# Attention with decay and a mixing layer: last tokens of two heads scored with a shared operand, and GpSimd's order fixed by more edges

## The chip, the cores and the metric

One core of a Trainium2 chip runs the whole program. Five engines work side by side, each through its own instructions in order: TensorE (PE in the profile; its weight loads are PEld), VectorE (DVE), ScalarE (ACT), GpSimd (POOL) and SyncE (SP, which here only issues DMAs). They hand work to each other by semaphores. The metric is the device time of one execution in microseconds; the kernel before has a median of 1192.06 us over three runs (1191.97 to 1192.15).

## The reference

Eight batches, eight heads, 576 tokens, head size 64. First attention with a decay for each head, then a mixing layer over tokens, then a two-layer network, all in f32:

```
scores = q @ k.T / 8                      # per batch and head, 576 x 576
cum    = cumsum(log(clip(f, 1e-4, 1)))    # per batch and head, 576
scores = where(causal, -1e9, scores + cum[:, None] - cum[None, :])
attn   = softmax(scores) ; x = attn @ v   # heads side by side: (8, 576, 512)
u      = x + (U V mixing over the 576 tokens)
out    = u + relu(u @ w_ch1) @ w_ch2      # 512 -> 2048 -> 512
```

A softmax row does not change when a constant is added to the row.

## The kernel before

**Numbers.** Products that need f32 accuracy are either one f32 matmul (pairs 0 to 5) or split into a rounded high part and a low part (f32r), and several f32r matmuls are added in one bank.

**The pair loop (9 to 643 us of the profile).** Two heads of a batch are a pair; there are 32 pairs. `step(t)` scores pair p = t, turns the probabilities of pair t-1 and multiplies them with values, and finishes pair t-2. A step has ten slots. Slots 0 to 3 score the first head (j = 0) in four blocks of 128 queries (`score`, 128 to 512 keys), slots 4 and 5 score the last 64 queries of both heads together in two halves of 288 keys (`score_tail`, HW = 288), the end of slot 6 to slot 9 score the second head (j = 1). Each score goes through VectorE (`top`: mask and negated maximum, L388 and L414) and ScalarE (`use`: exponential, L396 and L424). From pair NF = 6 on, a step also carries pieces of the mixing layer and of the first six of 16 chunks of the two-layer network (`filler`). After the loop the other ten chunks follow, which nothing here touches.

**Operands of the scores.** For pairs 0 to 5, q and k lie in `padded` tiles: rows 0 to 63 the head, two more rows the decay, the rest zero. `qk_mm` makes one f32 matmul of it (L364). From pair 6 on, tile G[j] (128 rows, 4 chunks, 640 columns) holds head j: chunk 0 the rounded q (L367 multiplies it with chunk 2, rounded k with the low part of k in the other rows), chunk 1 the low part of q with the decay of the queries in four rows, chunk 3 the rounded k with the decay of the keys (L368). `parts(p, j)` writes G[j]: two casts of 128x576 (ScalarE, in the step of a mix GpSimd), a cast of 64x576 (L330), and two subtractions of 64x576 on GpSimd, L345 (low part of k) and L346 (low part of q). G[0] for the next pair is written from slot 6, G[1] from slot 0. `place_decay` sends the decay rows by DMA (L351) at slot 7 for j = 0, at slot 0 for j = 1. `score_tail` puts four matmuls into a bank in each half: L367 and L368 for each head.

**Who sets the order.** TensorE and SyncE run in the order of the program text in most of the loop; VectorE, ScalarE and GpSimd in an order that a planner gives them, with extra edges by `behind` (a dependency without a semaphore). `at(phase, fn)` puts work into this slot, `defer(phase, fn, n)` n slots later, both ahead of the slot's loads and matmuls. On SyncE a DMA that waits holds all that is behind it.

**Mixing.** After the last pair of a batch, ten units (`mix_units`) run over one step: five `hmix`, four `tu` (transposes of the mixed tokens, split into uh and ul), one `tv`. For batches 1 to 6, `tu(2)` and `tu(3)` are staged: ScalarE copies the block to `full`, and GpSimd casts and subtracts it two slots later (L688, L689). Three slots after `tv`, uh and ul (1 MB each) are stored to `ud` for the sweep after the loop; odd batches store 256 KB more of each. `make_vs` splits the values, its low part on GpSimd (L199). `split_x` splits x (L630, L631 on GpSimd).

Of the kernel before, what the change touches and what calls it, by code (L numbers as in the profile page):

```python
# [21 lines left out]
P = 128  # L22
# [16 lines left out]
NF = 6  # L39


@with_exitstack
def tile_decay_attention_moe(ctx, tc, qk, v, f, U, V, w1, w2, out):
# [4 lines left out]
    accd = nc.dram_tensor("accd", (NG, NM, P, DM), F32, kind="Internal").ap()  # L48

# [5 lines left out]
    def behind(ins, kind):  # L55
        tc.add_manual_dep(
            ins.ins, newest[kind].ins.name,
            mybir.DependencyInfo(mybir.DependencyClass.NoSync, mybir.DependencyReason.DATA), reason=f"order behind {kind}",
        )
# [68 lines left out]
    mask = att.tile([P, ZR + HW], F32, name="mask")  # L128
    nc.vector.memset(mask, 0.0)
# [12 lines left out]
    def clear_operands():  # L142

        for j in range(2):
            g = G[j].bitcast(F32)
            tc.keep_in_program_order(nc.gpsimd.memset(g[OTH[j], 1, COLS[j]], 0.0))
            tc.keep_in_program_order(nc.gpsimd.memset(g[OTH[j], 3, COLS[j]], 0.0))
            tc.keep_in_program_order(nc.gpsimd.memset(g[ORW[j] : ORW[j] + 4, 1, COLS[j]], 1.0))
            tc.keep_in_program_order(nc.gpsimd.memset(g[ORW[j] : ORW[j] + 4, 3, COLS[j]], 1.0))
# [4 lines left out]
    def decay_log():  # L154
        fr = sb.tile([B * H, S], F32, tag="xT", name="fr")
        fl = sb.tile([B * H, S], F32, tag="cr", name="fl")
        return fr, fl, G[0][0 : B * H, :, 0:S], sb.tile([B * H, 2, S], F32, tag="VS", name="dq")
# [36 lines left out]
    def split(dh, dl, src, heng, leng):  # L194
# [4 lines left out]
        leng.tensor_tensor(dl, src, dh.bitcast(F32), op=ALU.subtract)  # L199
# [12 lines left out]
    def load_w(u):  # L212
# [4 lines left out]
        if kind == "w2":  # L217

            spare = xn[NX - 1].rearrange("p c d -> p (c d)").bitcast(I32)
            if fc % 2:  # L220
                raw, a = spare[:, 1536:2560], sb.tile([P, 512], I32, tag="w2a", name=f"stg{u}")
# [101 lines left out]
    def make_vs(p):  # L323
# [3 lines left out]
        split(VS[:, :, :, 0:D], VS[:, :, :, D:P], vr, nc.scalar, nc.gpsimd)  # L327
# [4 lines left out]
    def parts(p, j, engines):  # L332
# [46 lines left out]
    def score(p, j, i):  # L379
# [7 lines left out]
        def top():  # L387
            newest["top"] = nc.vector.tensor_tensor_reduce(  # L388
                ps[:, :w], ps[:, :w], mask[:, 512 - w : 512], scale=-SCALE, scalar=3.0e38,
                op0=ALU.add, op1=ALU.min, accum_out=z["nm"][:, col : col + 1],  # L390
            )

# [12 lines left out]
    def score_tail(p, x):  # L405
# [160 lines left out]
    def values(p, j):  # L566
# [7 lines left out]
        z["cr"] = sb.tile([D, S], F32, tag="cr", name=f"cr{p}_{j}")  # L574
# [1135 lines left out]
```

## Time and profile before

| | us |
|---|---|
| median of three runs | 1192.06 |
| profiled execution | 1192.27 |
| its span, first to last instruction | 1190.5 |
| TensorE busy | 1173.5 (99%) |
| VectorE, ScalarE, GpSimd busy | 906.1, 752.7, 561.1 |
| granted TensorE clock, mean | 1.000 of full |
| bytes moved | 138.47 MB, 116 GB/s |

Busy time counts from an instruction's start to its end; TensorE's matmuls overlap, so what one costs is read from the distance between starts. A timeline row gives start, length, engine, line, operation, output<-inputs and how many were merged; in brackets the idle time of the engine ahead of it and what ended it. The chain that ended last lies on TensorE for 85% of the span, on VectorE for 8%, on ScalarE for 4%.

### The profile page before, as it was taken

The numbers are of one execution on the slowest core, as the hardware profiler recorded it, in microseconds if no ns is written. First come the engines' busy times: TensorE is split into PE (matmuls) and PEld (weight loads), VectorE is DVE, ScalarE is ACT, GpSimd is POOL, SyncE is SP. The second block draws the span as 40 slices with busy tenths as digits, with TensorE's granted clock in tenths as the row PEclk, the third lists the DMA queues.
The fourth block names the chain that finished last, engine by engine and source line by source line (L and its number), as shares of the span: only waits on it lengthen the run. The fifth ranks groups of instructions, "written<-read, shape, count | busy, mean of one in ns | idle before, by whom it ended". The sixth has DMA issues, their size and how long they took to land.

```text
span 1190.5 us, 23774 instructions
## 1 busy us (share of the span) xinstructions
PE 1173.5 (99%) x8400; PEld 1080.8 (91%) x8400; DVE 906.1 (76%) x2188; ACT 752.7 (63%) x2046; POOL 561.1 (47%) x588
## 2 busy tenths in 40 slices
PE   8999999999999999999999999999999999999998
PEld 5888899999899989989989997788999999999998
DVE  8988777677777677777676699966777767777675
ACT  8887786766868758767765577344454544545443
POOL 3315565546637447555553000024565555555554
PEclk9999999999999999999999999999999999999999
DMA  5754234434426425426332344542424344243421
GB/s 161 196 147 153 78 98 146 116 82 142 121 74 174 114 58 163 111 74 179 82 84 96 108 142 155 155 112 95 131 89 124 97 135 138 94 107 102 130 54 36
DMA packets 81431, 138.47 MB, mean 116 GB/s; under 512 B 8768, under 2 KB 46144, under 8 KB 79264
## 3 DMA queue, kind: packets, MB, share of 16 engines
q1 hardware_dynamic: 79680, 128.16, 36.1%
q0 software_dynamic: 1152, 8.39, 3.8%
q8 instruction: 66, 1.08, 0.4%
q14 instruction: 53, 0.43, 0.1%
q10 hardware_dynamic: 480, 0.40, 0.1%
HBM read 101.08 MB, written 35.78 MB: 115 GB/s over the span
## 4 chain that ended last, share of the span: by engine, by line
PE 85%; DVE 8%; ACT 4%; issue 2%; POOL 1%; DMA 0%; SPq 0%; ACTq 0%; DVEq 0%; POOLq 0%
PE N L1321 12%; PE B L775 12%; PE A L756 11%; PE A L1301 9%; PE B L1301 7%; PE V L579 6%; PE T L467 4%; PE S L367 3%; PE S L368 3%; PE O L1402 2%; PE B L1321 2%; PE V L544 2%; PE Tt L645 2%; PE S L364 1%; PE T_v L485 1%
## 5 line engine op out<-in xcount | busy, mean ns | idle before, releaser
L396 ACT ACTIVATE P<-S,nm 128x128 f32<-128x128 f32 (+3 forms) x256 | 138.0, 541 | 53.7 <-DVE nm L388 52.7
L199 POOL TENSOR_TENSOR hb<-xn,hb 128x256 fp32r<-128x256 f32 x136 | 111.6, 840 | 126.3 <-ACT hb L196 113.4
L388 DVE CUSTOM_DVE_ANT_0 S<-S,mask 128x128 f32<-128x128 f32 (+3 forms) x256 | 125.7, 497 | 52.5 <-PE S L368 48.6
L330 POOL CAST G<-qk 64x576 fp32r<-64x576 f32 (+1 forms) x76 | 50.6, 679 | 172.4 <-PE St L368 63.8
L756 PE MATMUL A<-uh,w1h 128*128 128x256 f32 (+1 forms) x384 | 119.8, 312 | 0.0
L756 PE MATMUL A<-ul,w1h 128*128 128x256 f32 (+1 forms) x384 | 113.6, 296 | 0.0
L756 PE MATMUL A<-uh,w1l 128*128 128x256 f32 (+1 forms) x384 | 113.5, 296 | 0.0
L196 ACT CAST hb<-xn 128x256 fp32r<-128x256 f32 x136 | 51.7, 404 | 84.7 <-DVE xn L1307 45.5
L775 PE MATMUL B<-w2h,hh 128*128 128x512 f32 x216 | 88.2, 408 | 0.0
L446 DVE TENSOR_TENSOR PTl<-T,PTh 128x512 fp32r<-128x512 f32 (+1 forms) x156 | 78.4, 527 | 9.6 <-ACT PTh L443 8.6
L467 PE MATMUL T<-ident,P 128*128 128x128 f32 x544 | 85.3, 272 | 0.0
L775 PE MATMUL B<-w2l,hh 128*128 128x512 f32 x216 | 85.0, 394 | 0.0
L775 PE MATMUL B<-w2h,hl 128*128 128x512 f32 x216 | 84.6, 392 | 0.0
L1321 PE MATMUL N<-sw,hb 128*128 128x256 f32 x546 | 79.9, 282 | 0.0
L1321 PE MATMUL N<-b2h,hb 128*128 128x256 f32 x420 | 79.8, 282 | 0.0
L345 POOL TENSOR_TENSOR G<-qk,G 64x576 fp32r<-64x576 f32 x52 | 74.7, 1437 | 10.8 <-issue 4.1
L346 POOL TENSOR_TENSOR G<-qk,G 64x576 fp32r<-64x576 f32 x52 | 75.0, 1442 | 6.6 <-ACT G L330 5.0
L367 PE MATMUL S<-G 128*128 128x128 f32 x208 | 70.9, 345 | 4.5 <-ACT P L396 3.3
L756 PEld LDWEIGHTS A<-uh,w1h 128*128 128x128 f32 x384 | 72.9, 190 | 0.9 <-DVE hl L761 0.2
L756 PEld LDWEIGHTS A<-uh,w1l 128*128 128x128 f32 x384 | 73.1, 190 | 0.5
L756 PEld LDWEIGHTS A<-ul,w1h 128*128 128x128 f32 x384 | 72.9, 190 | 0.0
L1321 PEld LDWEIGHTS N<-sw,hb 128*128 128x128 f32 x546 | 71.6, 190 | 0.0
(342 smaller groups left out, 3995.1 us busy)
## 6 DMA issues: line engine op xcount, KB each, us to landing
qk<-in_qk_dram SPq DMA_DIRECT2D x104, 288.0 KB
direct<-ud SPq DMA_DIRECT2D x48, 256.0 KB
sr<-in_w_dram SPq DMA_DIRECT2D x20, 512.0 KB
vr<-in_v_dram SPq DMA_DIRECT2D x32, 256.0 KB
accd<-ost SPq DMA_DIRECT2D x32, 256.0 KB
xn<-accd SPq DMA_DIRECT2D x8, 1024.0 KB
out_dram<-xn SPq DMA_DIRECT2D x30, 256.0 KB
ud<-uh SPq DMA_DIRECT2D x7, 1024.0 KB
```

The source lines that it names most:

```text
L199: leng.tensor_tensor(dl, src, dh.bitcast(F32), op=ALU.subtract)
L345: pin(el.tensor_tensor(g[oth, 2, cols], k[oth], gf[oth, 2, cols], op=ALU.subtract))
L346: pin(em.tensor_tensor(g[own, 1, cols], q[own], gf[own, 0, cols], op=ALU.subtract))
L367: nc.tensor.matmul(ps, G[j][:, 0, c0 : c0 + P], G[j][:, 2, cols], start=first, stop=False)
L388: newest["top"] = nc.vector.tensor_tensor_reduce(ps[:, :w], ps[:, :w], mask[:, 512 - w : 512], scale=-SCALE, scalar=3.0e38, op0=ALU.add, o ...
L396: nc.scalar.activation(pt, ps[:, :w], AF.Exp, bias=z["nm"][:, col : col + 1], scale=-1.0, accum_out=z["sm"][:, col : col + 1])
L446: defer(2, lambda: nc.vector.tensor_tensor(dstl, src, dsth.bitcast(F32), op=ALU.subtract))
L467: nc.tensor.transpose(tp[:, P * x : P * x + P], z["P"][j][i][:, P * c : P * c + P], ident)
L756: nc.tensor.matmul(ps[:, :nt], wt[:, fc, c], ut[:, c, sl], start=m == 0, stop=m == 3 * NDC - 1)
L775: nc.tensor.matmul(ps, ht[:, fc, P * x : P * x + P], wt[:, fc], start=fc == 0 and m == 0, stop=fc == NA - 1 and m == 2,)
L1301: nc.tensor.matmul(ps, a[x][:, c], b[y][:, c], start=start and m == 0, stop=m == 5, skip_group_check=not start)
L1321: nc.tensor.matmul(ps[:, y], a[p_][:, P * y : P * y + P], w[q_], start=start and y == 0 and m == 0, stop=stop and y == 1 and m == 2,)
```

## The change

Six edits, all within the pair loop and what prepares it.

1. *Last tokens, pairs 6 to 31.* One matmul less per half. For each head the rounded q meets chunk 2 as before (two matmuls). The two products of the low parts of q become one: `join_keys` copies, by two DMAs at slot 0, head 0's rounded k into the other rows of G[1]'s chunk 3, and head 0's low q of the last tokens into chunk 1 beside head 1's. The decay rows of head 1's keys are overwritten by this; `place_decay` parks them in four spare rows of G[0] (`ASIDE`), and `next_decay` has GpSimd copy them over in slots 5 and 6, when the last tokens are scored.
2. *Last tokens, pairs 4 and 5.* `join_tail` has GpSimd put both heads' q and k into `both_q` and `both_k` (four copies), and one f32 matmul per half replaces two.
3. *Their decay.* From pair NO = 4 on the decay of the last tokens' keys comes in with the mask that VectorE adds: `based` (in DRAM, made once) holds -8 (cum - cum[511]); `load_tail` sends it to 64 rows for each head at slot 8 of the step before, and `lean_mask` has GpSimd add the causal part of the last 64 columns at slot 2. The decay of the queries, a constant in each row, is left out.
4. *Order on GpSimd.* `parts` notes its two subtractions as "lows"; the low part of VS and the casts of the staged blocks are put behind them. The staged blocks come 5 and 9 slots after their copy instead of 2 and 2.
5. *Stores.* uh and ul are stored 10 slots after `tv` instead of 3.
6. *Value sum.* `joined` (VectorE's sum of the two value halves) is put ahead of the maximum of the first head's second block (slot 1).

The tiles of the preparation change places with this (`fr`, `fl`, the staged w2 weights), the mask grows by 288 columns, and five of the ten memsets of `clear_operands` fall away. The core of the diff:

```diff
     def behind(ins, kind):
-        tc.add_manual_dep(ins.ins, newest[kind].ins.name, ...)
+        found = newest[kind]
+        for x in found if isinstance(found, tuple) else (found,):
+            tc.add_manual_dep(ins.ins, x.ins.name, ...)
...
     def make_vs(p):
-        split(VS[:, :, :, 0:D], VS[:, :, :, D:P], vr, nc.scalar, nc.gpsimd)
+        low = split(VS[:, :, :, 0:D], VS[:, :, :, D:P], vr, nc.scalar, nc.gpsimd)
+        if p < NP - 1:
+            behind(low, "lows")
...
     def parts(p, j, engines):
-        pin(el.tensor_tensor(g[oth, 2, cols], k[oth], gf[oth, 2, cols], op=ALU.subtract))
-        pin(em.tensor_tensor(g[own, 1, cols], q[own], gf[own, 0, cols], op=ALU.subtract))
+        low = pin(el.tensor_tensor(g[oth, 2, cols], k[oth], gf[oth, 2, cols], op=ALU.subtract))
+        last = pin(em.tensor_tensor(g[own, 1, cols], q[own], gf[own, 0, cols], op=ALU.subtract))
+        newest["lows"] = low, last
+
+    def load_tail(p):
+        if not NO <= p < NP:
+            return
+        for j in range(2):
+            r = j * B * NHP + p
+            nc.sync.dma_start(lean[64 * j : 64 * j + 64], based[r : r + 1].broadcast_to([64, S]))
+
+    def join_tail(p):
+        if not NO <= p < NF:
+            return
+        for j in range(2):
+            q, k = st[p]["qk"][j]
+            at = AOFF[1] if j else MAIN
+            nc.gpsimd.tensor_copy(both_q[OWN[j], 64 * j : 64 * j + TAIL], q[0:64, at : at + TAIL])
+            nc.gpsimd.tensor_copy(both_k[OWN[j]], k[0:64])
+
+    def lean_mask(p):
+        if NO <= p < NP:
+            nc.gpsimd.tensor_tensor(lean[:, MAIN:S], lean[:, MAIN:S], tri, op=ALU.add)
+
+    ASIDE = slice(96, 100)
+
+    def next_decay(lo, hi):
+        nc.gpsimd.tensor_copy(G[1][0:4, 3, AOFF[1] + lo : AOFF[1] + hi], G[0].bitcast(F32)[ASIDE, 3, lo:hi])
+
+    def join_keys():
+        g, h = (x.bitcast(F32) for x in G)
+        nc.sync.dma_start(h[OTH[1], 3, COLS[1]], g[OWN[0], 3, COLS[0]])
+        nc.sync.dma_start(h[OTH[1], 1, 0:TAIL], g[OWN[0], 1, MAIN:S])
 
     def place_decay(p, j, cm=None):
-            nc.sync.dma_start(G[j].bitcast(F32)[o : o + 4, 1:4:2, COLS[j]], cumd[r])
+            g = G[j].bitcast(F32)
+            if j == 0:
+                nc.sync.dma_start(g[o : o + 4, 1:4:2, 0:MAIN], cumd[r][:, :, 0:MAIN])
+                nc.sync.dma_start(g[ASIDE, 3, 0:MAIN], cumd[B * NHP + p][:, 1, 0:MAIN])
+            else:
+                nc.sync.dma_start(g[o : o + 4, 1, P:], cumd[r][:, 0, TAIL:S])
...
     def score(p, j, i):           # in top()
+            if (j, i) == (0, 1) and "joined" in newest:
+                behind(ins, "joined")
...
     def score_tail(p, x):
-        for j in range(2):
-            qk_mm(ps[:, :hw], p, ATAIL[j], cols, j == 0, j == 1, j)
+        if p < NO:
+            for j in range(2):
+                qk_mm(ps[:, :hw], p, ATAIL[j], cols, j == 0, j == 1, j)
+        elif p < NF:
+            nc.tensor.matmul(ps[:, :hw], both_q, both_k[:, cols], start=True, stop=True)
+        else:
+            at = [slice(AOFF[j] + cols.start, AOFF[j] + cols.stop) for j in range(2)]
+            for j in range(2):
+                nc.tensor.matmul(ps[:, :hw], G[j][:, 0, ATAIL[j] : ATAIL[j] + P], G[j][:, 2, at[j]], start=j == 0, stop=False)
+            nc.tensor.matmul(ps[:, :hw], G[1][:, 1, 0:P], G[1][:, 3, at[1]], start=False, stop=True)
-                ps[:, :hw], ps[:, :hw], mask[:, x * ZR : x * ZR + hw], scale=-SCALE,
+                ps[:, :hw], ps[:, :hw], lean[:, hw * x : hw * x + hw], scale=-SCALE,
...
     def evac_u(dh, dl, src, late):
-                    nc.gpsimd.tensor_copy(dh, whole)
+                    behind(nc.gpsimd.tensor_copy(dh, whole), "lows")
-                defer(6, parts_of, 2)
+                defer(6, parts_of, 5 if late == 1 else 9)
...
     def tv():                     # the stores of uh and ul
-            defer(7, use, 3)
+            defer(7, use, 10)
...
     def step(t):
             if s == 0 and ps_ and p >= NF:
                 place_decay(p, 1)
+                join_keys()
+            if s == 2 and ps_:
+                at(5, lambda: lean_mask(p))
+            if s == 5 and ps_ and p >= NF:
+                at(5, lambda: next_decay(0, HW))
+            if s == 6 and ps_ and p >= NF:
+                at(5, lambda: next_decay(HW, MAIN))
+            if s == 9 and ps_:
+                at(5, lambda: join_tail(p + 1))
+            if s == 8 and ps_:
+                load_tail(p + 1)
```

## Rows read from the trace of the kernel before

**Rows 1.** The page: span, and busy time of TensorE, share, instructions.
```profile
span 1190.5 us, 23774 instructions
...
PE 1173.5 (99%) x8400; PEld 1080.8 (91%) x8400; DVE 906.1 (76%) x2188; ACT 752.7 (63%) x2046; POOL 561.1 (47%) x588
```

**Rows 2.** Busy us by step: length, PE, PEld, DVE, ACT, POOL, clock, DMA share, GB/s.
```profile
62.53:77.83 15.30, 15.30 (x110) 12.84 (x108) 14.36 (x43) 12.03 (x37) 1.92 (x3) 1.00 0.51 149
...
303.74:322.44 18.70, 18.70 (x122) 16.69 (x121) 14.07 (x43) 15.01 (x44) 11.11 (x11) 1.00 0.38 98
...
sum 633.61, PE 625.05 PEld 564.46 DVE 487.12 ACT 472.70 POOL 326.48; mean PE 19.53 PEld 17.64 DVE 15.22 ACT 14.77 POOL 10.20
```

**Rows 3.** What TensorE waited for: us, times, longest.
```profile
PE S L367 <- ACT P L396: 3.3, 5, 1.1
```

**Rows 4.** Timeline of TensorE (start, us, what), one step: last-token scores.
```profile
312.15 0.29 PE L367 MATMUL St<-G 128*128 128x288 f32 x1
...
312.68 0.27 PE L507 MATMUL Ty<-ident,Ptl 128*64 128x128 f32 x1
...
317.08 0.22 PE L367 MATMUL S<-G 128*128 128x128 f32 x1
```

**Rows 5.** Timeline of TensorE, step of pair 4.
```profile
67.97 1.13 PE L364 MATMUL St<-qk 128*128 128x288 f32 x4
68.94 0.27 PE L507 MATMUL Ty_None<-ident,Ptl 128*64 128x128 f32 x1
```

**Rows 6.** Instructions of line 367: min/median/max ns.
```profile
L367 PEldq EVENT_SEMAPHORE  x26: 51/51/51, 90.4 to 621.1; - x26
```

**Rows 7.** Timeline of SyncE's issues.
```profile
298.43 6.16 SPq L351 DMA_DIRECT2D G<-cumd  x2
304.64 1.18 SPq L294 DMA_DIRECT2D qk<-in_qk_dram  x2
```

**Rows 8.** Engines and DMA (last two: share, GB/s) during a store of uh.
```profile
287.50:291.00 3.50, 3.50 (x29) 3.33 (x28) 3.02 (x9) 2.66 (x10) 3.42 (x3) 1.00 0.98 333
```

**Rows 9.** DMA issues: count, KB each, us to landing where it shows.
```profile
ud<-uh SPq DMA_DIRECT2D x7, 1024.0 KB
...
xn<-ud POOLq DMA_DIRECT2D x7, 1024.0 KB, 8.3
```

**Rows 10.** Timeline of GpSimd, a step after mixing and a plain one.
```profile
299.17 1.43 POOL L345 TENSOR_TENSOR G<-qk,G 64x576 fp32r<-64x576 f32 x1
...
313.39 0.66 POOL L330 CAST G<-qk 64x576 fp32r<-64x576 f32 x1 [4.33 <-PE St L368]
...
315.62 1.29 POOL L631 TENSOR_TENSOR xl<-xn,xh 128x512 fp32r<-128x512 f32 x1
...
318.61 1.43 POOL L345 TENSOR_TENSOR G<-qk,G 64x576 fp32r<-64x576 f32 x1
```

**Rows 11.** Timeline of VectorE, plain step.
```profile
306.52 0.43 DVE L388 CUSTOM_DVE_ANT_0 S<-S,mask 128x256 f32<-128x256 f32 x1
...
307.04 0.75 DVE L599 TENSOR_TENSOR xT<-V,cr 64x576 f32<-64x576 f32 x1
```

**Rows 12.** Timeline of GpSimd, a mixing step and the start of the next.
```profile
276.00 1.88 POOL L330 CAST G<-qk 128x576 fp32r<-128x576 f32 x3 [9.91 <-PE St L367]
...
278.49 1.29 POOL L631 TENSOR_TENSOR xl<-xn,xh 128x512 fp32r<-128x512 f32 x1
...
286.09 1.29 POOL L689 TENSOR_TENSOR ul<-full,uh 128x512 fp32r<-128x512 f32 x1
```

**Rows 13.** Timeline of GpSimd, the step after mixing of an odd batch.
```profile
211.85 1.44 POOL L345 TENSOR_TENSOR G<-qk,G 64x576 fp32r<-64x576 f32 x1
```

**Rows 14.** Timeline of TensorE, the step behind that one.
```profile
224.85 0.29 PE L367 MATMUL St<-G 128*128 128x288 f32 x1
```

**Rows 15.** Timeline of TensorE, the mixing step of rows 12.
```profile
276.18 0.60 PE L485 MATMUL T_v<-ident,Ptl 128*128 128x128 f32 x4
...
278.01 0.33 PE L367 MATMUL S<-G 128*128 128x128 f32 x1
```

More of the change, by code (lines that the diff above doesn't have):

```diff
@@ L39 @@
 NF = 6
+NO = 4
 @with_exitstack
@@ L48, in tile_decay_attention_moe @@
     accd = nc.dram_tensor("accd", (NG, NM, P, DM), F32, kind="Internal").ap()
+    based = nc.dram_tensor("based", (B * H, S), F32, kind="Internal").ap()
     def words(ap):
@@ L55, in behind @@
     def behind(ins, kind):
[L56 to L59, printed above, removed]
+        found = newest[kind]
+        for x in found if isinstance(found, tuple) else (found,):
+            tc.add_manual_dep(
+                ins.ins, x.ins.name,
+                mybir.DependencyInfo(mybir.DependencyClass.NoSync, mybir.DependencyReason.DATA), reason=f"order behind {kind}",
+            )
     def decode(raw, a, h, l, eng, rows=slice(0, 128), keep=False, sub=nc.gpsimd, halves=(0, 1)):
@@ L127, in tile_decay_attention_moe @@
     COLS = tuple(slice(o, o + S) for o in AOFF)
-    mask = att.tile([P, ZR + HW], F32, name="mask")
-    nc.vector.memset(mask, 0.0)
+    mask = att.tile([P, ZR + S], F32, name="mask")
+    nc.vector.memset(mask[:, 0:640], 0.0)
+    lean = mask[:, ZR:]
+    tri = att.tile([P, TAIL], F32, name="tri")
+    both_q = att.tile([P, P], F32, name="both_q")
+    both_k = sb.tile([P, S], F32, tag="xT", name="both_k")
     blank = mask[:, 0:256].bitcast(mybir.dt.bfloat16)
@@ L154, in decay_log @@
     def decay_log():
-        fr = sb.tile([B * H, S], F32, tag="xT", name="fr")
-        fl = sb.tile([B * H, S], F32, tag="cr", name="fl")
+        fr = sb.tile([P, 640], F32, tag="xh", name="fr")[0 : B * H, 0:S]
+        fl = sb.tile([P, S], F32, tag="cr", name="fl")[0 : B * H]
         return fr, fl, G[0][0 : B * H, :, 0:S], sb.tile([B * H, 2, S], F32, tag="VS", name="dq")
@@ L198, in split @@
             heng.tensor_copy(dh, src)
-        leng.tensor_tensor(dl, src, dh.bitcast(F32), op=ALU.subtract)
+        return leng.tensor_tensor(dl, src, dh.bitcast(F32), op=ALU.subtract)
     def w1_src(fc):
@@ L220, in load_w @@
             if fc % 2:
-                raw, a = spare[:, 1536:2560], sb.tile([P, 512], I32, tag="w2a", name=f"stg{u}")
+                raw, a = spare[:, 1536:2560], sb.tile([P, S], I32, tag="cr", name=f"stg{u}")[:, 0:512]
             else:
@@ L387, in top @@
         def top():
-            newest["top"] = nc.vector.tensor_tensor_reduce(
+            ins = newest["top"] = nc.vector.tensor_tensor_reduce(
                 ps[:, :w], ps[:, :w], mask[:, 512 - w : 512], scale=-SCALE, scalar=3.0e38,
@@ L598, in values, with joined @@
         defer(1, lambda: nc.scalar.copy(cr, pv[D:P, X0 : X0 + S]))
-        defer(4, lambda: nc.vector.tensor_tensor(xT[OWN[j]], pv[0:D, X0 : X0 + S], cr, op=ALU.add))
+        def joined():
+            newest["joined"] = nc.vector.tensor_tensor(xT[OWN[j]], pv[0:D, X0 : X0 + S], cr, op=ALU.add)
+        defer(4, joined)
     def turn_x(p):
@@ L822, in tile_decay_attention_moe @@
         pad(1, 0)
+        nc.gpsimd.memset(mask[:, 640:], 0.0)
         nc.gpsimd.affine_select(mask[:, DG : DG + P], mask[:, DG : DG + P], [[-1, P]], ALU.is_ge, MASKED, base=0, channel_multiplier=1)
@@ L825, in tile_decay_attention_moe @@
             nc.gpsimd.affine_select(
-                mask[64 * j : 64 * j + 64, ZR + HW - TAIL :], mask[64 * j : 64 * j + 64, ZR + HW - TAIL :],
+                lean[64 * j : 64 * j + 64, MAIN:S], lean[64 * j : 64 * j + 64, MAIN:S],
                 [[-1, TAIL]], ALU.is_ge, MASKED, base=0, channel_multiplier=1,
@@ L848, in tile_decay_attention_moe @@
         load_w(3)
+        nc.gpsimd.tensor_copy(tri, lean[:, MAIN:S])
+        nc.gpsimd.memset(both_q, 0.0)
+        nc.gpsimd.tensor_scalar(fl, fr, fr[:, MAIN - 1 : MAIN], -8.0, op0=ALU.subtract, op1=ALU.mult)
+        nc.sync.dma_start(based, fl)
     mixing = []
```

7 lines of the change are left out of this document (3 added, 4 removed).

## The prediction

> **What bounds the kernel now.** I read the page's engine shares first, then the busy times by step, then what TensorE waits for, then the timelines of TensorE, GpSimd, SyncE and VectorE in a few steps of the pair loop. The profiled execution took 1192.27 us, 1.77 more than its span; the three runs have a median of 1192.06, 0.2 less. A difference worked out in the span is taken off the median. TensorE is busy 1173.5 of 1190.5 us [rows 1]. That alone proves no bound, so the second view matters: over the 32 steps of the pair loop (9 to 643 us) TensorE is idle for 633.61 - 625.05 = 8.6 us in all, VectorE for 146 and GpSimd for 307 [rows 2]. The largest wait that TensorE has for another engine in the whole kernel is 3.3 us, in five waits for ScalarE's exponentials [rows 3]. So in this loop a TensorE instruction taken out is time taken out, unless what replaces it comes late. That is the question here: the change takes a little work out of TensorE and puts new hand-overs (DMA, GpSimd) right beside the matmuls that stay.
>
> **The matmuls that go.** Pairs 6 to 31 score their last tokens with four matmuls of 288 columns per half. A half's four start at 312.15 and the next instruction at 312.68 [rows 4]: 0.53 us, or 0.1325 each, not the 0.29 that a row shows, for they overlap. Now there are three per half: 2 x 26 x 0.1325 = 6.9 us less. Pairs 4 and 5 use f32 matmuls of two instructions each; four instructions run from 67.97 to 68.94 [rows 5], 0.97 us a half. One matmul of two goes: 4 halves x 0.485 = 1.9 us. Gross 8.8 us. In pair 4's step VectorE is busy 14.36 of 15.30 us [rows 2], so of that pair's 0.97 us between nothing and all may turn into waiting for VectorE; I charge 0.3. At the five places where TensorE waits for exponentials already [rows 3], the 0.265 us saved in a pair may just lengthen the wait: 0 to 1.3, taken 0.3, since a later slot can still use what an earlier one saved.
>
> **Waits that come.** The third matmul of a half waits for two copies between the G tiles, and the first score of the second head for GpSimd's copy of the decays. Some waits stand in TensorE's queue as instructions of their own; L367 has 26 of these, 51 ns each [rows 6]. Two more per pair are 52 x 0.051 = 2.7 us if each shows, nothing if the queue runs ahead; I take 1.0.
>
> **The copies (join_keys).** SyncE issues them at slot 0 behind place_decay of the second head, which is held until the last score of the pair before has run and whose issue ends at 298.43 + 6.16 = 304.59 [rows 7]. Behind them stand load_qk and all later loads, none of which is wanted in the same step. An issue takes 1.18 / 2 = 0.59 us [rows 7], so the second copy is issued from 305.2. The matmul that wants it starts at 312.15 + 2 x 0.1325 = 312.4 [rows 4]: 7.2 us of room. No row shows such a copy (147 KB) land. From below it is its bytes at 333 GB/s [rows 8], 0.4 us; from above the 8.3 us of a 1 MB load on GpSimd's queue [rows 9], which would be 1.1 us late in each of 26 pairs, 29 us. Of these 8.3 us 3.1 are bytes, so the nearest value is 8.3 - 3.1 + 0.4 = 5.6 us: no wait, nothing charged. In all SyncE gets five more issues per pair (two copies, two mask loads, one decay row), 3 us of a 19 us step, hidden in its waiting.
>
> **GpSimd.** Per pair it gets two decay copies of 4 rows (288 and 224 columns) and one 128x64 add. The 64x576 cast takes 0.66 and the 128x512 subtraction 1.29 [rows 10]; by columns that is 0.6 + 0.2, with their starts some 0.9 us (0.5 to 1.5). It is busy 11.1 of 18.7 us in such a step [rows 2], and when TensorE ends the last-token scores it stands idle: the cast at 313.39 had waited 4.33 us for just that [rows 10]. So the first copy starts at about 312.7, the second at 313.4, and the score that needs the first starts at 317.08 [rows 4]: nothing. The casts and subtractions behind end 0.9 us later, at 320.9 instead of 318.61 + 1.43 = 320.0 [rows 10], and the next pair's first score is at 322.4, where that step ends [rows 2]: nothing. The edges that put VS and the staged blocks behind the subtractions free a queue whose lateness is not among TensorE's large waits; nothing (bounds -3.3, all the waits of rows 3, and +1). The copies for pairs 4 and 5, and the memsets that are dropped, fall in or beside pair 4's step, where GpSimd is busy 1.92 of 15.30 us [rows 2].
>
> **The value sum ahead of a maximum.** VectorE takes the maximum at 306.52 and the value sum at 307.04 [rows 11]. Swapped, the maximum comes later by the sum's 0.75 and up to 0.5 of waiting. Its bank is wanted again two slots on, so nothing (bounds 0 and 0.4 in a few steps). The sum being early is worth nothing, as TensorE has no large wait for it.
>
> **The stores that move.** The 1 MB stores of uh and ul go out ten slots after tv, in the last slot of the step after mixing and so just ahead of the next pair's place_decay and join_keys. GpSimd's second staged block now follows the subtractions: 299.17 + 1.43 [rows 10] + 0.9 = 301.5, its cast (0.6) to 302.1, its subtraction (1.29, [rows 12]) to 303.4. Two stores of 1 MB at 333 GB/s [rows 8] take 6.3 us: to 308.4 at the best, the copies to 308.9, and starting and landing on top, 0 to 5.2 us (the 8.3 less its bytes), against 312.4. Odd batches store 0.5 MB more: 211.85 + 1.44 [rows 13] + 0.9 + 0.6 = 214.8, 7.9 us of bytes to 222.7, copies to 223.1 plus 0 to 5.2, against 224.85 + 0.27 = 225.1 [rows 14]. Five steps have such stores ahead of their copies (batches 1 to 5). With 2.4 us for starting and landing, near the middle, the three odd ones wait 0.4 us: 1.2 us in all.
>
> The Trainium skill has a rule that speaks against this place: by its page DMA: Bandwidth & Descriptors, section Queues, rings and completion order, each DMA engine consumes the descriptors of one issuing engine in ring order, and a semaphore is raised only after that DMA engine's earlier writes. By the rule the copies can't overtake the stores and the 1.2 us above stands; without it they wouldn't wait and the sum would be 1.2 us better. The trace shows the DMA engines 98% busy during such a store [rows 8], and no row here shows the order.
>
> **The sum.** -6.9 - 1.9 + 0.3 + 0.3 + 1.0 + 1.2 = -6.0 us: 1192.06 - 6.0 = **1186.0 us**.
>
> **Rivals.** *Copies behind the stores.* Starting and landing take 3.5 us, or GpSimd's block is 1.1 us later than worked out: 1.5 us at the three odd steps, nothing yet at the two even ones: 4.5 instead of 1.2, 1189.3 us. For it: the stores fill all DMA engines [rows 8]. Against: it needs the upper half of a bound taken from another queue.
> *Nothing late, and old waits go.* The charges of 2.8 us fall away, and with them 2 of the 8.6 idle us: 1192.06 - 8.8 - 2 = 1181.3 us. For it: GpSimd's queue becomes clearer where it was fullest. Against: TensorE has no large wait for GpSimd that could go.
> *GpSimd's decay copies come late; slower.* GpSimd runs its instructions in the order that the planner gives them, and two copies that wait for TensorE now stand among casts and subtractions. If they come behind the casts and the split of x, the first ends in a mixing step at 278.49 + 1.29 + 0.4 = 280.2 [rows 12], while TensorE wants it at 278.01 + 0.1, 1.9 us after the last-token scores end at 276.18 [rows 15]: 2.1 us in seven such steps, 15 us; in plain steps at 315.62 + 1.29 + 0.4 = 317.3 [rows 10] against 317.1, 0.2 x 19 = 4. Then 1186.0 + 19 = 1205 us. It decides from the point where the first copy ends after that score's start; at about 0.9 us late in the seven the gain is gone. For it: the room in the mixing steps. Against: what the copies wait for comes before what the casts wait for, and the casts at 276.00 found the queue empty for 9.91 us [rows 12].
>
> **Chances.** Forecast 0.60 (its own range 1182.5 to 1188.5), copies behind the stores 0.17, old waits gone 0.13, GpSimd late 0.10. A measurement of this kernel tells some 0.2% (2.4 us) from no change; faster by more is below 1189.7: nearly all of the first, half of the second, and the third: 0.80. Within 0.2%: the other half and a little of the first and last: 0.11. Slower: 0.09. The range takes in the old waits gone and most of the copies' case, 1181.0 to 1191.0, and leaves out GpSimd late and the worst landings.
>
> **What would show it.** Right: 156 last-token matmuls in pairs 6 to 31 instead of 208, still 0.13 us apart; TensorE waits for no DMA there; steps shorter by 0.27 us. Wrong: St waiting for the copies in the steps after stores (the first rival), S waiting for GpSimd's decay copies (the last), or new waits for ScalarE and VectorE of over 3 us in sum, which would mean that the loop was balanced and not bound by TensorE.

## The result, and the profile after

The changed kernel takes 1208.94 us (median of 4 runs, 1208.27 to 1211.42) beside 1192.05 (1191.97 to 1192.15) for the kernel before: a ratio of 1.0145 (1.0133 to 1.0158). The forecast was 1186.0. It is slower by 16.9 us where 6.0 less were expected. Two executions of the kernel before, beside experiments 9 to 11, took 1624 us at a mean granted clock of 0.654; no ratio below rests on them.

First the page after, which answers to [rows 1]: the span, and TensorE's busy time, share and instructions.

```profile
span 1206.4 us, 24092 instructions
PE 1173.4 (97%) x8340; PEld 1074.1 (89%) x8340; DVE 908.6 (75%) x2188; ACT 752.1 (62%) x2046; POOL 595.1 (49%) x675
```

There are 60 matmul instructions fewer, as worked out (2 x 26 and 4 x 2), yet TensorE is busy just as long. The sum over the whole kernel hides that some steps gain and others lose. The stretch from the pair loop's first score to the first matmul of the network's part behind the loop is clearer. The columns are those of [rows 2]. The first two rows are of the kernel before: the whole stretch, and step 17, a plain step. The next three are after: the whole stretch, step 16 and step 17.

```profile
9.39:721.18 711.79, 703.15 (x4858) 634.75 (x4859) 549.90 (x1528) 521.87 (x1459) 329.80 (x336) 1.00 0.43 121
322.44:341.44 19.00, 19.00 (x159) 18.56 (x157) 14.83 (x46) 15.81 (x48) 10.52 (x10) 1.00 0.37 96
```

```profile
9.40:737.24 727.84, 703.16 (x4798) 628.08 (x4799) 553.65 (x1528) 521.54 (x1459) 361.71 (x421) 1.00 0.48 136
309.87:331.43 21.56, 19.22 (x120) 16.46 (x119) 14.11 (x43) 14.90 (x43) 13.47 (x15) 1.00 0.62 176
331.44:350.19 18.75, 18.75 (x156) 18.29 (x155) 14.62 (x46) 15.95 (x48) 11.62 (x13) 1.00 0.46 122
```

The profiled spans differ by 15.9 us, and this stretch by 727.84 - 711.79 = 16.05: the whole difference lies here. Step 17 became 0.25 us shorter, just as forecast (0.265), and so did TensorE's busy time in it. Step 16, which stands in [rows 2] at 18.70, now takes 21.56, and TensorE is idle for 2.3 of it and busy 0.5 longer. So the gain is there in each undisturbed step, and a few steps lose much more. The start of each step's first score gives all the step lengths. In the table, "after" and two experiments stand as differences from before; the last line is the sum of the groups. The 32nd step is counted up to the end of the stretch above.

```
steps                              after   stores later   without the edge
12, 16, 20, 24, 28 (after stores) +12.68      +0.41           -1.21
11, 15, 23, 27                     +3.39      +3.26           +0.18
3 to 7                             +4.06      +2.57           +2.31
the other 18                       -4.08      -2.91           -4.35
all 32                            +16.05      +3.34           -3.07
```

What TensorE waits for, after (us, times, longest), beside [rows 3]:

```profile
PE St L467 <- DMA G<-G: 9.8, 5, 3.0
PE S L414 <- ACT P L445: 7.4, 14, 1.4
```

The copies between the G tiles were to cost nothing by themselves and 1.2 us behind the stores; five waits for them cost 9.8 us. The waits for exponentials grew from 3.3 us in five to 7.4 in fourteen. These are the two mechanisms of the loss in the later steps; the early steps 3 to 7 are a third place.

**The first mechanism, in step 16.** GpSimd after, around the second staged block (cast L749, subtraction L750):

```profile
305.22 1.42 POOL L354 TENSOR_TENSOR G<-qk,G 64x576 fp32r<-64x576 f32 x1
306.70 0.61 POOL L749 CAST uh<-full 128x512 fp32r<-128x512 f32 x1
307.27 0.32 POOL L378 TENSOR_TENSOR mask<-mask,tri 128x64 f32<-128x64 f32 x1
310.16 0.66 POOL L339 CAST G<-qk 64x576 fp32r<-64x576 f32 x1 [2.57 <-issue]
310.79 1.42 POOL L355 TENSOR_TENSOR G<-qk,G 64x576 fp32r<-64x576 f32 x1
312.28 1.44 POOL L354 TENSOR_TENSOR G<-qk,G 64x576 fp32r<-64x576 f32 x1
313.68 1.29 POOL L750 TENSOR_TENSOR ul<-full,uh 128x512 fp32r<-128x512 f32 x1
```

SyncE, issues (start, us, what), and its waits for the same store in the whole kernel:

```profile
307.34 0.39 SPq L788 DMA_DIRECT2D ud<-uh  x1
315.00 0.39 SPq L788 DMA_DIRECT2D ud<-ul  x1
315.48 0.35 SPq L398 DMA_DIRECT2D G<-cumd  x1
315.88 0.49 SPq L387 DMA_DIRECT2D G<-G  x1
316.42 1.38 SPq L388 DMA_DIRECT2D G<-G  x1
```

```profile
SPq L788 <- POOL ul L750: 40.8, 6, 7.2
```

TensorE, the last-token scores of that step, which answer to [rows 4]:

```profile
318.32 0.43 PE L466 MATMUL St<-G 128*128 128x288 f32 x2
320.85 0.37 PE L467 MATMUL St<-G 128*128 128x288 f32 x1 [2.11 <-DMA G<-G]
```

Read them in this order. The block's cast runs at 306.70, right behind the subtraction that the new edge names. Its own subtraction has everything it needs at 307.3, and GpSimd then even stands idle for 2.57 us; but in the instruction order the next head's cast and two subtractions come first, so it ends at 314.97. SyncE stands at the store of ul until then (7.3 us) with both copies behind it. The third matmul of the half, ready at 318.74, waits behind the store's 1 MB and the copies till 320.85. By its step the subtraction ends 5.1 us after the start (309.87) and not 0.3 before it, as forecast (303.4 against 303.74).

The 6.4 us between the end of that cast and the start of its subtraction are not the edge's work. GpSimd runs the second cast and the second subtraction nearly as far apart in the kernel before (5.8 us, cast L688, subtraction L689), and just as far in experiment 10, which has no edge on the casts (6.4 us):

```profile
285.52 0.61 POOL L688 CAST uh<-full 128x512 fp32r<-128x512 f32 x1
291.90 1.28 POOL L689 TENSOR_TENSOR ul<-full,uh 128x512 fp32r<-128x512 f32 x1
```

```profile
286.44 0.62 POOL L749 CAST uh<-full 128x512 fp32r<-128x512 f32 x1
293.42 1.28 POOL L750 TENSOR_TENSOR ul<-full,uh 128x512 fp32r<-128x512 f32 x1
```

What the edge sets is the place of the cast: 3.2 us before the step's start with it, 17.9 without it (304.30 in experiment 10).

**The second mechanism, in step 15.** VectorE, then GpSimd, after:

```profile
291.42 1.33 DVE L494 TENSOR_SCALAR sm<-sm 128x9 f32<-128x9 f32 x1 [0.92 <-ACT P L445]
292.79 0.22 DVE L495 RECIPROCAL rv<-sm 128x9 f32<-128x9 f32 x1
...
374.98 0.21 DVE L494 TENSOR_SCALAR sm<-sm 128x9 f32<-128x9 f32 x1 [0.92 <-ACT P L445]
```

```profile
291.29 1.44 POOL L355 TENSOR_TENSOR G<-qk,G 64x576 fp32r<-64x576 f32 x1
...
375.12 1.44 POOL L355 TENSOR_TENSOR G<-qk,G 64x576 fp32r<-64x576 f32 x1
```

Adding 1e-9 to nine columns takes 0.21 us in step 19, where it starts just ahead of GpSimd's subtraction, and 1.33 us in step 15, where it starts 0.13 us behind it; it ends at 292.75, with that subtraction (292.73). VectorE's next maximum stands behind it, then ScalarE's exponential, and TensorE waits for that one:

```profile
293.86 0.44 PE L414 MATMUL S<-G 128*128 128x384 f32 x1 [0.22 <-ACT P L445]
```

The addition is held in the same way at 200.54, 465.31 and 548.96 (1.31, 1.26 and 1.23 us): steps 11, 23 and 27. Set beside experiment 4, which has no such addition and in these steps the same matmuls, TensorE falls 0.68 to 0.79 us behind in each of the four steps within 1.1 us of the start of this wait, and hardly anywhere else in them: 2.9 us together. The Trainium skill, page GPSIMD Engine Reference, section Specifications, says that GpSimd's SBUF interfaces are shared with VectorE, with contention for VectorE instructions in a 2-port mode or with two SBUF inputs. The trace agrees that there is contention. The addition has one SBUF input, and no run here shows whether it runs in a 2-port mode. What these rows show is that it is held until GpSimd's instruction has ended, and ends 0.03 us after it.

### The profile page after: what moved, and what is told of

It is laid out like the page before. It is cut to its first block, busy times and chain, and to the rows that moved or that the text cites. A ratio compares the mean times of both kernels' runs of the same rounds, so it can differ in the third digit from the quotient of the medians.

```text
span 1206.4 us, 24092 instructions
## 1 busy us (share of the span) xinstructions
PE 1173.4 (97%) x8340; PEld 1074.1 (89%) x8340; DVE 908.6 (75%) x2188; ACT 752.1 (62%) x2046; POOL 595.1 (49%) x675
## 4 chain that ended last, share of the span: by engine, by line
PE 76%; DVE 11%; ACT 5%; issue 3%; DMA 2%; POOL 1%; SPq 1%; ACTq 0%; DVEq 0%; POOLq 0%
PE N L1398 12%; PE A L817 10%; PE B L836 9%; PE A L1378 9%; PE B L1378 7%; PE V L636 4%; PE T L524 3%; PE S L414 2%; PE O L1479 2%; PE B L1398 2%; PE S L415 2%; PE V L601 2%; PE S L411 1%; PE Tt L706 1%; DMA G<-G 1%
```

## Experiments

All times are medians, with the ratio to the kernel before run on the same chip.

**1. The stores one slot later** (SyncE then issues them behind the copies).

```diff
-            defer(7, use, 10)
+            defer(7, use, 11)
```

> The changed kernel with one number different: the stores of uh and ul go out 11 slots after tv instead of 10, so SyncE issues the next pair's decay row and the two copies between the G tiles ahead of them. Theory (the copies are late since SyncE waits for the store of ul, which waits for GpSimd's second half of the staged block, 11.5 us later than I worked out, and then run behind 1 MB of store): TensorE's five waits for these copies (9.8 us) go, the five steps after stores come down by 12 to 14 us in all, 1195 +- 1.5 us. Rival (the copies are late because they read and write SBUF while much else moves, whatever stands ahead of them): the waits stay within 2 us of 9.8 and the time is above 1205.

Measured: 1195.92 us, 1.0035 (1.0022 to 1.0048). The waits for G<-G are gone and the five steps are back within +0.41 of before. 13 of the 17 us go with the place of the stores. What is left is in steps 11, 15, 23, 27 and 3 to 7, unchanged in place.

**2. The lean scores alone**, without the edges, the later blocks, the later stores and the value sum's order.

```diff
-            behind(low, "lows")
-                behind(ins, "joined")
-                    behind(nc.gpsimd.tensor_copy(dh, whole), "lows")
+                    nc.gpsimd.tensor_copy(dh, whole)
-                defer(6, parts_of, 5 if late == 1 else 9)
+                defer(6, parts_of, 2)
-            defer(7, use, 10)
+            defer(7, use, 3)
```

> The changed kernel without its edits 4 to 6: last tokens scored the new way, but the staged blocks 2 slots after their copy, the stores 3 slots after tv, no edges behind the subtractions and none for the value sum. Theory (the loss lies in the moved stores and in how GpSimd's queue falls against VectorE, and not in the scoring): no wait for the copies, 1186 to 1193 us. Rival (the new hand-overs of the scoring cost more than its matmuls save, wherever the stores go): 1197 or more.

Measured: 1196.69 us, 1.0049 (1.0032 to 1.0066): between both. The copies cost nothing, but a wait appears that neither theory had, TensorE for the value sum:

```profile
PE S L412 <- ACT P L441: 5.0, 7, 1.4
PE T_v L520 <- DVE xT L654: 3.3, 8, 0.6
```

The changed kernel, which has the value sum ahead of the maximum, has no such wait. That this order removes it was not tested by itself.

**3. The orders alone**, on the kernel before: the same five lines the other way round.

```diff
+            behind(low, "lows")
+                behind(ins, "joined")
+                    behind(nc.gpsimd.tensor_copy(dh, whole), "lows")
+                defer(6, parts_of, 5 if late == 1 else 9)
+            defer(7, use, 10)
```

> The kernel before with edits 4 to 6 alone: GpSimd's order, staged blocks 5 and 9 slots late, stores 10 slots after tv, value sum ahead of the maximum; last tokens scored as before, so no copies that could stand behind the stores. Theory: there is nothing that waits for the stores but the decay row, which is wanted later; 1190 to 1195 us. Rival (the order itself starves TensorE): 1198 or more.

Measured: 1198.2 us, 1.0051 (1.0036 to 1.0066). The rival held. The old scores read a decay row that SyncE loads at the same place, behind the stores:

```profile
308.96 0.36 SPq L738 DMA_DIRECT2D ud<-ul  x1
309.42 0.67 SPq L356 DMA_DIRECT2D G<-cumd  x1
```

```profile
314.23 0.40 PE L373 MATMUL St<-G 128*128 128x288 f32 x1 [1.45 <-DMA G<-cumd]
```

Here too the block's subtraction (L700) ends 5.1 us after the start of step 16. So the late block and the held SyncE come from the orders, with or without lean scores; the lean scores put a larger transfer there. This run also has the small addition held for 1.19 to 1.21 us in steps 11, 15, 23 and 27, and these four steps are 0.36 us shorter in sum than before. In step 15 the addition starts 1.81 us into the step here, and 2.20 in the changed kernel, and TensorE has no wait in these four steps. So in these runs the hold costs time only where the exponential behind it comes too late for TensorE.

**4. Without the 1e-9** on the softmax sums (that part of the computation is left out).

```diff
-        nc.vector.tensor_scalar(sm[:, 0:9], sm[:, 0:9], 1e-9, None, op0=ALU.add)
```

> The changed kernel without VectorE's addition of 1e-9 to the row sums (128x9), which leaves out that part of the reference; the sums are at least 1. In steps 11, 15, 23 and 27 this little operation takes 1.23 to 1.33 us instead of 0.17 to 0.35 and ends with GpSimd's subtraction that started 0.1 us ahead of it. Theory (VectorE is held by GpSimd's two-input operation there, and it lies on the path to the exponentials for which TensorE then waits): these four steps become 0.8 to 1.7 us shorter and step 7 about 1 us; 1203.5 to 1205.5 us. If the reciprocal behind it is held in its place, nothing is won. Rival (those steps are long because ScalarE is late by itself): within 1 us of 1208.9.

Measured: 1205.39 us, 1.0113 (1.0098 to 1.0128): 3.5 us less for an instruction of 0.2 us. Steps 11, 15, 23 and 27 go from +3.39 to +0.49, steps 3 to 7 from +4.06 to +1.49; the waits for the copies stay (9.5 us).

**5. The second staged block two slots earlier**, stores where the change put them.

```diff
-                defer(6, parts_of, 5 if late == 1 else 9)
+                defer(6, parts_of, 5 if late == 1 else 7)
```

> The changed kernel with one number different: GpSimd's second staged block comes 7 slots after its copy instead of 9, so that its subtraction stands ahead of the next pair's casts and subtractions in GpSimd's queue; the stores stay where the change put them, ahead of the copies. Theory (it is the lateness of that block, 315 instead of 303 in the step I worked out, and not the place of the stores as such, that makes the copies late): the five waits for the copies shrink from 9.8 to under 3 us in all, 1198 to 1201.5 us. Rival (1 MB of store ahead of the copies is too much even when it starts in time): waits of 7 us and more, above 1204.

Measured: 1197.91 us, 1.0049 (1.0032 to 1.0065), a little better than the range. The waits for the copies are gone and the five steps are 0.22 to 0.26 shorter than before. In step 16 the subtraction ends 2.4 us before the start. The place of the stores is harmless as long as the block is in time.

**6. Stores later, and pairs 4 and 5 as before.**

```diff
-NO = 4
+NO = 6
-            defer(7, use, 10)
+            defer(7, use, 11)
```

> The kernel with the stores one slot later (1195.92 us, runs from 1195.4 to 1198.3) with pairs 4 and 5 scored as before (NO = 6). Theory (scoring these two pairs the new way saves 1.9 us of TensorE, and loses as much since GpSimd's copies and two more loads per pair come where DMA is fullest; the loss differs from run to run): 1195.0 to 1197 us, steps 3 to 5 together 45.2 us and the runs within 0.6 us of each other. Rival (the new scoring of these pairs is a gain, and the spread is from elsewhere): 1197.5 or more, with as wide a spread.

Measured: 1194.36 us (1193.51 to 1197.73), 1.0017 (1.0008 to 1.0027). Lower than expected, and the runs lie as far apart as with pairs 4 and 5 lean: the spread does not need them.

**7. Lean scores with the value sum's order, without the 1e-9** (left out), on the kernel of experiment 2.

```diff
+            if (j, i) == (0, 1) and "joined" in newest:
+                behind(ins, "joined")
-        nc.vector.tensor_scalar(sm[:, 0:9], sm[:, 0:9], 1e-9, None, op0=ALU.add)
```

> Edits 1 to 3 as in the run with these alone (1196.69 us), with the value sum ahead of the maximum (edit 6), and without VectorE's addition of 1e-9, which leaves out that part of the reference. In the run with edits 1 to 3 alone TensorE waited 3.3 us in eight places for the value sum, and VectorE was held in the little addition for 11.6 us in all. Theory (both are real losses of that run): the waits for xT go, 1189 to 1192 us. Rival (each wait that goes is replaced by one for the next operation in line): 1194 or more.

Measured: 1193.99 us (1190.36 to 1197.44), 1.0016 (1.0003 to 1.0028). The waits for the value sum are gone, but the 1e-9 is too, so the run does not show which of the two took them away; a wait for the decay row is new (1.3 us in three). The time is 2.7 us less than in experiment 2, and leaving out the 1e-9 alone gave 3.5 in experiment 4: a gain in time by the order is not shown. The median is at the rival's edge, with the widest spread of all.

**8. Stores later, without the 1e-9** (left out).

```diff
-        nc.vector.tensor_scalar(sm[:, 0:9], sm[:, 0:9], 1e-9, None, op0=ALU.add)
-            defer(7, use, 10)
+            defer(7, use, 11)
```

> The kernel with the stores one slot later (1195.92 us) without VectorE's addition of 1e-9, which leaves out that part of the reference. The two losses found so far, copies behind the stores and VectorE held by GpSimd, lie in different steps, so they should add: theory 1195.92 - 3.5 = 1192.4, 1191 to 1193.5 us. Rival (they share a cause, and without the first the second costs nothing): within 1 us of 1195.9.

Measured: 1191.89 us, 0.9998 (0.9989 to 1.0008). The two losses add: 13.0 + 3.5 off 1208.94 make 1192.4.

**9. As 8, with the early part undone too** (1e-9 left out): pairs 4 and 5 as before, the joined tiles gone, the rates' tile back in its old place.

```diff
-NO = 4
+NO = 6
-        fr = sb.tile([P, 640], F32, tag="xh", name="fr")[0 : B * H, 0:S]
+        fr = sb.tile([B * H, S], F32, tag="xT", name="fr")
-    both_q = att.tile([P, P], F32, name="both_q")
-    both_k = sb.tile([P, S], F32, tag="xT", name="both_k")
```

> The changed kernel with the stores one slot later, without the 1e-9 that is added to the softmax sums, with pairs 4 and 5 scored as before (NO = 6, the two joined tiles and their copies gone), and with the rates' tile back in the place it had before. Theory: what the lean version still loses comes from the preparation, where tiles moved for this change and the added copies and loads make the first value loads and weight decodes late (steps 3 to 7 of the loop cost 1.9 us more in the kernel with stores later and no 1e-9, 1189.7 us in its profiled span): the early steps go back to 0.3 us of before, 1187 to 1190 us, and the runs lie within 1.5 us. Rival: the early loss comes from the extra traffic and waits that any version with loads of mask rows has, or from the granted clock after any small wait there: 1190.5 to 1193 us, runs still 2 to 4 us apart.

Measured: 1190.17 us (1189.5 to 1192.53), 0.9987 (0.9978 to 0.9996). The time lies 0.17 us above the theory's range and below the rival's, and the theory's reason does not hold: steps 3 to 7 together still cost +1.7 (1.9 in experiment 8), and the runs are 3 us apart. The profile of this one is better mainly at step 20. So what was undone here is not what the early steps lose most by.

**10. The changed kernel without the edge on the staged blocks**, all else kept.

```diff
-                    behind(nc.gpsimd.tensor_copy(dh, whole), "lows")
+                    nc.gpsimd.tensor_copy(dh, whole)
```

> The changed kernel without the order edge that puts GpSimd's staged blocks behind the operand differences (the block still nine slots after its copy, VS still behind, stores where the change put them). Theory: the second block's subtraction is late because nine slots put its due time into the same stretch as the next pair's casts and subtractions, whatever the edge: the matmuls for the last tokens still wait for the copies behind the stores, 9 to 14 us in five steps, 1203 to 1210 us. Rival: the edge itself makes it late; without it the block runs in GpSimd's idle time, the waits go, and the time is 1195 to 1199 us.

Measured: 1189.97 us (1189.13 to 1191.61), 0.9984 (0.9975 to 0.9993). My theory fell and the rival held, and by more than it said: with all else as the change has it the edge costs 19 us, and without it the change is 2.1 us faster than the kernel before. GpSimd, then SyncE, in the same stretch:

```profile
291.29 1.56 POOL L206 TENSOR_TENSOR VS<-vr,VS 128x640 fp32r<-128x640 f32 x1
292.80 0.66 POOL L339 CAST G<-qk 64x576 fp32r<-64x576 f32 x1
293.42 1.28 POOL L750 TENSOR_TENSOR ul<-full,uh 128x512 fp32r<-128x512 f32 x1
...
299.75 1.41 POOL L354 TENSOR_TENSOR G<-qk,G 64x576 fp32r<-64x576 f32 x1
```

```profile
299.85 0.51 SPq L788 DMA_DIRECT2D ud<-ul  x1
304.49 0.26 SPq L398 DMA_DIRECT2D G<-cumd  x1
304.80 0.53 SPq L387 DMA_DIRECT2D G<-G  x1
```

Step 16 starts at 304.30 here. The block's subtraction ends 9.6 us before it instead of 5.1 after, the store goes out as soon as SyncE reaches it, and the copies follow the start by half a microsecond. GpSimd's other work moved too, and with it the collisions on VectorE: in steps 11, 15, 23 and 27 the small addition takes 0.37 to 0.64 us here, where after has 1.23 to 1.33 and experiment 1 1.12 to 1.37. Its sums over the kernel (busy us, mean ns), after and without the edge:

```profile
L494 DVE TENSOR_SCALAR sm<-sm 128x9 f32<-128x9 f32 x32 | 14.4, 450 | 15.6 <-ACT P L445 15.3
```

```profile
L494 DVE TENSOR_SCALAR sm<-sm 128x9 f32<-128x9 f32 x32 | 12.6, 395 | 13.8 <-ACT P L445 11.6 <-POOL G L339 1.8
```

The stretch as a whole and steps 16 and 17 of this kernel:

```profile
9.75:718.47 708.72, 696.91 (x4799) 626.32 (x4798) 553.05 (x1528) 521.47 (x1458) 361.00 (x420) 1.00 0.49 140
304.30:322.76 18.46, 18.46 (x120) 16.42 (x119) 13.90 (x43) 15.12 (x44) 11.20 (x12) 1.00 0.58 165
322.76:341.51 18.75, 18.75 (x156) 18.29 (x155) 14.70 (x46) 15.76 (x48) 12.59 (x15) 1.00 0.45 122
```

**11. The kernel before without the 1e-9** (left out): the control for 4, 7, 8 and 9.

```diff
-        nc.vector.tensor_scalar(sm[:, 0:9], sm[:, 0:9], 1e-9, None, op0=ALU.add)
```

> The kernel before without the 1e-9 that is added to the softmax sums (that part of the computation is left out). Control for the runs that leave it out. Theory: in the kernel before this small VectorE operation was held by GpSimd in only a few steps, which cost TensorE next to nothing: 1191 to 1192.2 us. Rival: it cost TensorE there as much as in the changed kernel, 3 us and more: 1189 us or less.

Measured: 1190.44 us, 0.9987 (0.9977 to 0.9996): 1.6 us less, between both. It gains in steps 0, 2 and 7 (0.74, 0.80 and 0.91), nothing in steps 11, 15, 19, 23 and 27. So of the 3.5 to 4.0 us that the instruction costs in the changed kernel, 1.6 were there before, and about 2 to 2.4 came with the change. Experiments 8 and 9 are therefore no gain of the change: they stand 1.5 above and 0.3 below this control.

**12. Without the edge and with the early part undone**, 1e-9 included: the early part of 9 and the edit of 10 together, stores where the change put them. (Of the early part the main lines are shown, here and in 9.)

```diff
-NO = 4
+NO = 6
-        fr = sb.tile([P, 640], F32, tag="xh", name="fr")[0 : B * H, 0:S]
+        fr = sb.tile([B * H, S], F32, tag="xT", name="fr")
-                    behind(nc.gpsimd.tensor_copy(dh, whole), "lows")
+                    nc.gpsimd.tensor_copy(dh, whole)
```

> The complete computation, 1e-9 included: the changed kernel without the order edge on GpSimd's staged blocks (that edge alone cost 19 us), stores where the change put them, and besides that pairs 4 and 5 scored as before (NO = 6, joined tiles gone) and the rates' tile back in its old place. Theory: the two undoings add up, as they act on different steps; the early steps gain some 0.5 us over the kernel without the edge (step 3 +0.7 instead of +1.3, step 5 +0.0 instead of -0.9, step 7 up to 0.9 less): 1188.5 to 1190 us, faster than the kernel before by 2 to 3.5 us. Rival: the joined scores of pairs 4 and 5 are worth what they cost, and the planner arranges the later steps otherwise again: 1190 to 1192 us, no better than without the edge alone.

Measured: 1190.42 us (1189.63 to 1192.4), 0.9989 (0.9980 to 0.9998). No better than 10: the rival held. Steps 3 to 7 cost +2.5, as in 10 (+2.3). The version to keep is 10.

## Why the prediction was wrong

**The step that failed** is in "The stores that move": "GpSimd's second staged block now follows the subtractions: ... its cast (0.6) to 302.1, its subtraction (1.29, [rows 12]) to 303.4". The cast came where I had put it: 306.70 is 3.2 us before its step's start, and I had 301.5, 2.2 before it. The subtraction did not come right behind it. I took cast and subtraction for one piece. In GpSimd's order four instructions stand between them, two subtractions of 64x576 among these, in the kernel before as well (286.13 to 291.90). With the edge the cast comes only at the end of the step before, and so the four are those of the next step: the addition to the mask, the next head's cast and two subtractions. The block ended 5.4 us later than forecast in step 16, and 4.4 in step 12 (224.75, 4.1 behind that step's start of 220.65; I had the cast end at 214.8 and so the subtraction at 216.1, 0.3 ahead of a start of 216.44). The rest of that sum was right in size in step 16: from the store's issue (315.00 + 0.39) with 3.1 us of bytes and 0.4 for the copies, 2.0 us remain to 320.85 for starting and landing, where I took 2.4. So 1.2 us became 13.9 (12.68, and five times the 0.25 that such a step should have gained). The rule of the Trainium skill cited there (DMA: Bandwidth & Descriptors, section Queues, rings and completion order) is one for each DMA engine; it does not by itself order whole transfers, as the prediction had it. The trace agrees as far as it goes: the wait for copies issued 0.9 us behind the store of ul lasted till 320.85, 5.9 us after the start of that store's issue. Experiments 1, 5 and 10 each remove these waits in another way: the place of the stores, the slots, the edge. It takes all three together to make them. Only without the edge does the rest pay too; half of the 6 us between experiments 1 and 10 lies in steps 11, 15, 23 and 27 (+0.18 instead of +3.26), where the small addition is held for less time.

**Copies behind the stores** was a rival with this mechanism, at 1189.3; it took the block 1.1 us late, and it was four to five times as late.

**The matmuls** that go: 0.265 us a pair was forecast; steps without a new wait mostly got 0.20 to 0.27. The two further semaphore waits, charged at 1.0 (0.04 in a pair), show as 0.015 at most in step 17: 0.25 instead of 0.265. Pairs 4 and 5 were to give 1.6 us net; experiments 10 and 12, with and without them, differ by 0.45 us in the median, which their runs (over 2 us apart) don't tell from nothing. VectorE, 14.36 of 15.30 us busy there [rows 2], is the reason I gave for the charge; that it takes all of it was not shown.

**The copies themselves and GpSimd's decay copies**: right. In a plain step nothing waits for either; the rival that had GpSimd's decay copies late named the right sign and the wrong place.

**The edges that put VS and the blocks behind the subtractions** were priced at nothing, with bounds of -3.3 and +1: the one on the blocks cost 19 us. I looked at what GpSimd's queue had as slack ahead of the subtractions, not at who stands behind a block that is put off.

**The value sum ahead of a maximum** was priced at nothing beside the kernel before, which is right; but experiment 2, without it, has 3.3 us in eight waits for the value sum that the changed kernel does not have.

**What I had no term for** is VectorE held by GpSimd: +3.39 us in steps 11, 15, 23 and 27 where 1.0 less was due, so 4.4 in all. Experiment 4 shows 2.9 of these to be the held addition; the rest stays open. GpSimd's new order made four of its subtractions start just ahead of the addition, and experiment 3 shows that this costs nothing with the old scores. I priced every GpSimd instruction by what waits for its result, and none by what runs beside it on VectorE.

**Open**: steps 3 to 7 (+4.06 after, +2.31 in experiment 10, with no row that names one cause) and the spread of the runs. Part of the first is this stretch after, in the columns of [rows 2]:

```profile
56.00:59.60 3.60, 2.49 (x23) 2.28 (x22) 2.79 (x10) 3.26 (x12) 3.14 (x7) 1.00 0.17 43
59.60:63.00 3.40, 3.40 (x15) 3.00 (x15) 2.19 (x5) 0.00 (x0) 2.45 (x3) 0.51 0.37 103
```

TensorE was idle for 1.1 us in the first window, and in the second its granted clock is 0.51, the 1.2 GHz level. It did 15 instructions in 3.40 us there. The profile of experiment 10 has an idle time of 1.05 us at the same place and no such stretch, and its step 3 is +1.27 where after has +2.98. What decides whether an execution gets one was not settled.

The spread has to do with such stretches, as two profiles show. That of experiment 5 (1199.99 us, the longest of four executions) has three, in steps 4 and 7, which are +1.98 and +3.58 where experiment 10 has -0.29 and +1.87. That of experiment 6 (1197.73 us, the longest of ten) has this one, and its step 3 is +5.47 where experiment 9 has +0.69:

```profile
59.55:66.38 6.83, 6.83 (x33) 6.12 (x33) 3.25 (x9) 0.47 (x3) 0.20 (x1) 0.50 0.06 14
```

In experiment 7 the three shortest executions (up to 1191.96 us) had a mean granted clock of 0.999 to 1.000, the five longest (from 1194.28) 0.995 to 0.997. The spread comes with the lean scores: experiment 3, with the orders alone, repeats within 0.1 us. The stretches are not all of it, for in experiment 12 one in step 7 leaves that step at +1.96, beside +1.87 without one in experiment 10.

The other part of the early steps is in step 7, the same after and in experiment 10: VectorE takes 1.85 us for a 128x512 weight subtraction (its ten others after take 0.63 to 0.99), beside a subtraction of GpSimd, and TensorE waits 1.2 us for what stands behind it.

```profile
131.62 0.69 DVE L503 TENSOR_TENSOR PTl<-T,PTh 128x512 fp32r<-128x512 f32 x1 [0.46 <-ACT PTh L500]
132.23 1.85 DVE L82 TENSOR_TENSOR w2l<-stg,w2h 128x512 fp32r<-128x512 f32 x1
```

```profile
132.12 1.41 POOL L354 TENSOR_TENSOR G<-qk,G 64x576 fp32r<-64x576 f32 x1
```

## What to carry to other kernels

An order edge that puts off the first of two paired instructions puts off the second as well, and the second need not stand right behind the first. How far apart they stand can be read from the trace of the kernel before (5.8 us here). Add that distance, and ask which in-order queue waits for the second one's result and with what behind it. Here one such edge cost 19 us, nine times what the change is worth without it (2.1). Test the edits one by one: three experiments took away one part each of the same chain and all made the waits go, and only the one on the edge left a kernel faster than before.

## What the hardware showed that was not expected

A VectorE instruction of 0.17 to 0.35 us (128x9, one SBUF input) takes up to 1.40 when it starts 0.13 to 0.40 us behind a two-input GpSimd instruction, and ends 0.03 us after it, in all five places of over 1.2 us after the change. In a kernel bound by TensorE, with VectorE only 75% busy, leaving that one instruction out gave 3.5 us after the change and 1.6 before it. Half the granted clock for 3.4 us appeared after an idle time of 1.1 us in one profile and not in another with nearly the same idle time. The kernel before has no such stretch in the loop of its profile. Executions of one kernel with the lean scores lie 2.5 to 7.1 us apart, those of experiment 3, with the orders alone, 0.1.
